# A first set of eight plain products, and the last tokens' turn moved at the border of two mixture layers

## The chip, the cores and the metric

The kernel runs on one core of a Trainium2 chip. The metric is device time in microseconds (us), the median of three runs; the kernel before takes 621.7 us.

The engines are named as in the profile: PE is TensorE (PEld its weight loads), DVE is VectorE, ACT is ScalarE, POOL is GpSimd, SP issues nearly all DMAs. Each engine works through its own queue in the order in which the program emits; semaphores hold an instruction until its operands are there and its output is free.

## The reference, cut to what matters

```python
# 1: retention with decay, batch 2, 8 heads, 576 tokens, head size 64
scores = (q @ k.T) / sqrt(64)
x1 = (scores * Dmat) @ v              # Dmat: gamma_h ** (i - j) for i >= j, else 0
x = x1 to (1152, 512)                 # tokens x model
# 2: four experts of 1024 hidden, weighted by normalized domain_probs
out = sum(p[:, e] * (relu(x @ w1[e]) @ w2[e]) for e in range(4))
# 3: one layer of 2048 hidden, weights in 64-bit floats
h = out @ w_in
y = (h * tanh(softplus(h))) @ w_out   # Mish
```

All is computed in 32-bit precision on TensorE's rounded 32-bit type: each operand is split into a high part (rounded by a copy on ScalarE) and a low part (the rest, by a subtraction), and a product is three matmuls: high x high, low x high, high x low.

## The kernel before

**Retention** (`retention`, L418 to L509). Eight units of one batch and one pair of heads, u = 0 to 7; unit u holds batch u % 2 of pair u // 2. In turn u TensorE computes scores(u), then the values of unit u - 1, the state of unit u, the last scores, and the cross step of unit u - 1. ScalarE scales the keys of unit u + 1 (`prep_k`, L301), copies the state (L363, the first step of `chain`), and places the finished unit in `acc` with its high parts (`place_x`, L403, L411). VectorE does the decay (L332), the rest of the chain (L365) and the low parts (`rest_x`, L416). GpSimd scales the queries of unit u + 1 (`prep_q`, L310, L315). After the loop come the values and the cross step of unit 7. `load_unit` (L273) queues a unit's keys, queries, values and constants (`cst_sb`) on SP.

**Weights.** A chunk (O: first layer, W: second layer) is loaded by `load_w` (L111) into one of three raw buffers and turned into high and low parts by `split_w` (L147): a copy on ScalarE (L153), then four quarter-size subtractions on GpSimd or one on VectorE (L157). A G chunk is made from the raw O chunk by `weight_sums` (L124): four operations on GpSimd (L129 to L132), in place, so its split reads what they leave. `tasks` (L166) is the list of such steps, and `weight_task` (L171) takes the next when it is called and the buffers allow it. In retention it is called once in turns 2, 3 and 6 and twice in turn 5; there it gives O00 split, G00 sums, G00 split, O01 split, G01 sums.

**The two layers** (`feed_forward`, L802). Twelve units of 512 hidden (u = 0 to 7 experts, 8 to 11 the Mish layer), in the order that `steps` (L52) writes out. The first 1024 tokens and the 512 model rows form a 2 x 2 grid of blocks B11, B12, B21, B22; a set S(u, c) (`first_pair`, L609) computes half a unit's hidden layer by seven products on sums of blocks (T1 to T4 of x, G of the weights) in place of eight, and combines them on VectorE and GpSimd. `hidden` (L597) applies ReLU or Mish and splits. The 128 last tokens take a path of their own: L(u, c) (`first_last`, L674), 12 products whose result VectorE transposes in blocks and SP turns by way of DRAM (`turn_rest`, L666, five DMAs). Y(u, c, tb) is a turn of the second layer (`m2`, L754), T(u) the last tokens' (`m2_t`, L779). The second layer's results leave from two PSUM buffers (`ps_tile`, L211) through VectorE (L764, L765).

**The first set** (S(0, 0)) starts inside retention: product 1 runs ahead of the cross step of unit 7 (L488), T sums and splits are spread over turns 3 to 6 and the end (`t_sum`, `t_high`, `t_rest`, L258 to L268).

**The border** lies between u = 7 and u = 8: x of the Mish layer is what the experts leave in `acc`, so its blocks are split (`x_split`, `hi`, `lo`) and its last tokens turned once more, while TensorE goes on to S(8, 0).

The order on each engine is the order of emission (`manual_schedule`, L200).

Of the kernel before, what the change touches and what calls it, by code (L numbers as in the profile page):

```python
# [13 lines left out]
ALU = mybir.AluOpType  # L14
# [5 lines left out]
P = 128  # L20
# [14 lines left out]
CG = 2 * P + D  # L35
KVW = 4 * W4 // P * D + D
CSTW = CG + P + 3
# [11 lines left out]
}  # L49

# [23 lines left out]
def retention_moe_mish(ctx: ExitStack, tc: tile.TileContext, kq_in, kv_in, probs, w1, w2, w64, cdec, out):  # L74
# [10 lines left out]
    order = [(m, 0, c) for m in "OG" for c in range(2)]  # L85
# [61 lines left out]
    def split_w(key, lo_engine, defer=False):  # L147
# [14 lines left out]
        if m != "O":  # L162
            n_raw_max[0] += 1
# [3 lines left out]
    o0, o1, g0, g1 = order[:4]  # L167
    tasks[:6] = [(False, o0), (True, g0), (False, g0), (False, o1), (True, g1), (False, g1)]
# [45 lines left out]
    def product(u, c, n, o):  # L214

        m, kh, fb, r, t, j, opens = PRODUCTS[n]
# [19 lines left out]
    ahead_of = {}  # L236
    early, later = [], []
# [5 lines left out]
    with ExitStack() as actx:  # L243
# [6 lines left out]

        dec_sb = cst_sb[:, :, CSTW - 3:]


        def t_parts(n, kk):
            b11, b12, b21, b22 = (acc[:, i + kk, j * TB:(j + 1) * TB] for i in (0, 2) for j in range(2))
            return {T1: (b11, b12, b11), T3: (b12, b22, b12), T2: (b22, b22, b11), T4: (b21, b21, b22)}[n]

        def t_sum(n, kk):  # L258
            out, a, b = t_parts(n, kk)
            dve.tensor_tensor(out=out, in0=a, in1=b, op=ALU.subtract)  # L260

        def t_high(n, kk):
            act.activation(out=xop[:, 0, n, kk], in_=t_parts(n, kk)[0], func=AF.Copy)

        def t_rest(n, kk):
            dve.tensor_tensor(
                out=xop[:, 1, n, kk], in0=t_parts(n, kk)[0], in1=f32(xop[:, 0, n, kk]), op=ALU.subtract
            )  # L268
# [4 lines left out]
        def load_unit(u):  # L273
# [14 lines left out]
            if b == 0 and u != 4:  # L288
                sp.dma_start(out=cst_sb[:, pr], in_=cdec[pr])
# [50 lines left out]
        def scores_last(u):  # L340
# [5 lines left out]
            for o in own:  # L346
# [3 lines left out]
                in1=cst_sb[:, units[u][1], 2 * P:CG], op=ALU.mult,  # L350
# [47 lines left out]
        def place_x(u, o):  # L398
# [520 lines left out]
```

## Time and profile before

| what | us |
|---|---|
| median of three runs (621.2 to 621.73) | 621.7 |
| the profiled execution | 621.62 |
| its span in the trace | 619.7 |
| TensorE busy in the span | 603.8 |
| VectorE busy | 442.6 |
| GpSimd busy | 377.0 |
| ScalarE busy | 312.9 |

The rows below are lines of one profiled execution. A timeline line gives the start and the length in us, the engine, the line of the kernel, the operation, output and input with shapes, and a count; in brackets stands how long the engine had been idle and what released it. Times count from the start of the span. In lines of the chain a piece is the time that this work held the end of the kernel.

### The profile page before, as it was taken

The page shows a single profiled execution, that of the slowest core. Times are in us where ns is not written, and L with a number is a line of the kernel's source. Part 1 is how long each engine was busy: PE and PEld are TensorE (multiplying, and loading weights), DVE is VectorE, ACT ScalarE, POOL GpSimd, SP SyncE. Part 2 cuts the span into 40 slices and gives each one's busy share as a digit, 9 for nine tenths or more (in the row PEclk, how much of TensorE's full clock was granted, in tenths as well). Part 3 has the DMA queues.
Part 4 walks back from the last instruction along what each step waited for, and adds up shares of the span by engine and source line. Part 5 has one row for each costly group of instructions (what it writes and reads, how often), then busy time and mean ns, then how long its engine had stood idle before and what let it go on. Part 6 is the DMA issues. An engine that isn't in the chain of part 4 may idle for free.

```text
span 619.7 us, 8570 instructions
## 1 busy us (share of the span) xinstructions
PE 603.8 (97%) x3183; PEld 498.5 (80%) x3183; DVE 442.6 (71%) x579; ACT 312.9 (50%) x478; POOL 377.0 (61%) x422
## 2 busy tenths in 40 slices
PE   8999999999999999999999999997899999999997
PEld 7976888888888888888888888875788788888885
DVE  3997768789779779689779779586676867344233
ACT  3676357446446446446446446315656665344120
POOL 2796748758748748758748748663361775854300
PEclk8999999999999999999999999998999999999999
DMA  8933306434523524523524623620220541220023
GB/s 334 400 114 100 120 0 203 121 105 141 162 98 126 152 88 145 175 85 129 160 86 130 195 86 111 178 51 17 48 91 15 172 136 52 85 69 1 0 68 120
DMA packets 56658, 72.30 MB, mean 117 GB/s; under 512 B 31144, under 2 KB 38312, under 8 KB 56616
## 3 DMA queue, kind: packets, MB, share of 16 engines
q1 hardware_dynamic: 56472, 71.46, 36.2%
q8 instruction: 25, 0.41, 0.3%
q10 hardware_dynamic: 144, 0.29, 0.1%
q14 instruction: 17, 0.14, 0.1%
HBM read 57.57 MB, written 14.17 MB: 116 GB/s over the span
## 4 chain that ended last, share of the span: by engine, by line
PE 76%; DVE 10%; DMA 6%; ACT 5%; issue 2%; SPq 1%; POOL 1%; DVEq 0%; ACTq 0%; POOLq 0%
PE b L220 31%; PE ps L695 26%; PE ps L711 14%; PE ps L679 4%; DMA kv<-kv_in 3%; DMA hs<-turned 1%; DMA turned<-hs 1%; DVE x L737 1%; ACT h L601 1%; DVE acc L260 1%; ACT b L600 1%; DVE b L617 1%; SPq L671 1%; DVE h L605 1%; DVE x L416 1%
## 5 line engine op out<-in xcount | busy, mean ns | idle before, releaser
L157 POOL TENSOR_TENSOR w<-wr,w 128x256 fp32r<-128x256 f32 x256 | 216.6, 877 | 119.3 <-ACT w L153 119.3
L220 PE MATMUL b<-x,w 128*128 128x512 f32 x1008 | 243.0, 398 | 7.2 <-DVE x L737 4.7
L220 PEld LDWEIGHTS b<-x,w 128*128 128x128 f32 x1008 | 189.0, 189 | 55.8 <-DVE x L737 6.2
L695 PE MATMUL ps<-h,w 128*128 128x512 f32 x768 | 176.9, 389 | 0.0
L695 PEld LDWEIGHTS ps<-h,w 128*128 128x128 f32 x768 | 143.0, 188 | 29.3 <-issue 0.3
L153 ACT ACTIVATE w<-wr 128x1024 fp32r<-128x1024 f32 x72 | 75.0, 1053 | 29.5 <-POOL wr L132 28.7
L711 PE MATMUL ps<-w,h 128*128 128x512 f32 x384 | 89.1, 390 | 0.3 <-DVE acc L798 0.2
L711 PEld LDWEIGHTS ps<-w,h 128*128 128x128 f32 x384 | 71.4, 188 | 16.0 <-POOL w L157 0.8
L232 ACT ACTIVATE p<-b 128x512 f32<-128x512 f32 x72 | 42.0, 596 | 55.1 <-PE b L220 55.0
L604 ACT ACTIVATE h<-b 128x512 fp32r<-128x512 f32 x64 | 38.2, 597 | 54.4 <-DVE b L617 45.3
L605 DVE SCALAR_TENSOR_TENSOR h<-b,h 128x512 fp32r<-128x512 f32 x64 | 42.7, 689 | 26.2 <-ACT h L604 25.1
L636 POOL TENSOR_TENSOR p<-p,p 128x512 f32<-128x512 f32 x24 | 35.1, 1461 | 36.2 <-ACT p L232 36.2
L764 DVE TENSOR_TENSOR ps<-ps,pb 128x1024 f32<-128x1024 f32 x28 | 34.4, 1229 | 19.3 <-PE ps L695 19.3
L617 DVE TENSOR_TENSOR b<-b,p 128x512 f32<-128x512 f32 x72 | 47.5, 690 | 0.5 <-PE b L220 0.2
L602 DVE TENSOR_TENSOR h<-b,h 128x512 fp32r<-128x512 f32 x32 | 22.1, 690 | 29.3 <-ACT h L601 29.3
L553 ACT ACTIVATE e<-e,cbias 128x512 uint32<-128x512 uint32 x32 | 22.9, 717 | 34.1 <-DVE e L541 34.1
L679 PEld LDWEIGHTS ps<-w,xc 128*128 128x128 f32 x288 | 37.2, 188 | 2.1
L679 PE MATMUL ps<-w,xc 128*128 128x256 f32 x288 | 37.6, 279 | 0.0
L567 DVE TENSOR_TENSOR g<-g,e 128x512 f32<-128x512 f32 x32 | 35.4, 1107 | 1.1
L564 DVE SCALAR_TENSOR_TENSOR g<-w,g 128x512 f32<-128x512 uint32 x32 | 36.0, 1125 | 0.0
L617 DVE TENSOR_TENSOR p<-b,p 128x512 f32<-128x512 f32 x24 | 16.5, 686 | 26.9 <-PE b L220 18.4
L711 PE MATMUL ps<-w,hl 128*128 128x512 f32 x144 | 35.0, 391 | 0.6 <-DVE hl L605 0.6
(81 smaller groups left out, 609.6 us busy)
## 6 DMA issues: line engine op xcount, KB each, us to landing
wr<-w SPq DMA_DIRECT2D x32, 512.0 KB, 5.1
w<-w SPq DMA_DIRECT2D x32, 512.0 KB, 4.5
O<-g SPq DMA_DIRECT2D x16, 256.0 KB, 5.3
W<-g SPq DMA_DIRECT2D x16, 256.0 KB, 4.1
wr<-O SPq DMA_DIRECT2D x8, 512.0 KB, 3.7
wr<-W SPq DMA_DIRECT2D x8, 512.0 KB, 3.3
kq<-kq_in SPq DMA_DIRECT2D x7, 576.0 KB, 9.8
kv<-kv_in SPq DMA_DIRECT2D x7, 544.0 KB, 9.4
```

What stands on the lines that cost most here:

```text
L153: act.activation(out=w[:, 0], in_=t, func=AF.Copy)
L157: lo_engine.tensor_tensor(out=w[:, 1, k], in0=t[:, k], in1=f32(w[:, 0, k]), op=ALU.subtract)
L220: pe.matmul(o[t][j], w[:, a, 2 * kh + kk, fb * P:(fb + 1) * P], xop[:, b, r, kk], start=opens and kk == 0 and i == 0, stop=kk == 1 and i == 2,
L232: act.activation(out=t, in_=src, func=AF.Copy)
L564: dve.scalar_tensor_tensor(out=g, in0=lo_w, scalar=2.0 ** -52, in1=g, op0=ALU.mult, op1=ALU.add)
L567: dve.tensor_tensor(out=g, in0=g, in1=e.bitcast(F32), op=ALU.mult)
L604: act.activation(out=out[:, 0], in_=src, func=AF.Relu)
L605: dve.scalar_tensor_tensor(out=out[:, 1], in0=src, scalar=0.0, in1=f32(out[:, 0]), op0=ALU.max, op1=ALU.subtract)
L617: dve.tensor_tensor(out=out, in0=a, in1=b, op=ALU.add)
L679: pe.matmul(o, xc[:, b, k], w[:, a, k], start=k == 0 and n == 0, stop=k == 3 and n == 2)
L695: pe.matmul(o[:, j], w[:, a, d:d + P], h[:, b, f], start=i == f == n == 0, stop=i == f == 1 and n == 2,)
L711: pe.matmul(o[:, n], h, w[:, b, f * DM:(f + 1) * DM], start=k == f == i == 0, stop=k == f == 1 and i == 2,)
```

## The change

The first set S(0, 0) is computed as eight plain products (list `PLAIN`, `first_plain`) and not as seven on sums. The G weights of this half, the T sums inside retention and the product ahead of the last cross step go; `place_x` also makes the parts of B12, in T4's place. T1, T3, T2, T4 are made from `t_first` around the set. The calls of `weight_task` in turn 3 go, and the list begins O00, O01, G01 sums, G01 split. The first unit's constants are loaded in two pieces, the second behind the keys and queries of unit 1. In every product the two matmuls with the low part of x come last. At the border, L(7, 1) moves into S(7, 1) behind product 6, the last tokens' hidden step ahead of Y(7, 0, 0), no weight is loaded in the steps of Y(7, 0, 0) and Y(7, 0, 1), the split of the turned last tokens goes from Y(7, 1, 1) into S(8, 0) behind product 1, the low part of B21 goes to GpSimd, and S(8, 0) finishes product 3's sums with product 2's.

```diff
+PLAIN = [
+    ("O", 0, 1, B11, 0, 1, True), ("O", 0, 1, T4, 1, 1, True),
+    ("O", 0, 0, B11, 0, 0, True), ("O", 0, 0, T4, 1, 0, True),
+    ("O", 1, 0, B21, 0, 0, False), ("O", 1, 1, B21, 0, 1, False),
+    ("O", 1, 0, B22, 1, 0, False), ("O", 1, 1, B22, 1, 1, False),
+]
...
-    order = [(m, 0, c) for m in "OG" for c in range(2)]
+    order = [("O", 0, 0), ("O", 0, 1), ("G", 0, 1)]
...
-        if m != "O":
+        if m != "O" or key[1:] == (0, 0):
...
-    o0, o1, g0, g1 = order[:4]
-    tasks[:6] = [(False, o0), (True, g0), (False, g0), (False, o1), (True, g1), (False, g1)]
...
-        for kk in range(2):
-            for i, (a, b) in enumerate(((0, 1), (0, 0), (1, 0))):
-                pe.matmul(
-                    o[t][j], w[:, a, 2 * kh + kk, fb * P:(fb + 1) * P], xop[:, b, r, kk],
-                    start=opens and kk == 0 and i == 0, stop=kk == 1 and i == 2,
-                    skip_group_check=not opens,
-                )
+        terms = [(kk, a, 0) for kk in range(2) for a in range(2)] + [(kk, 0, 1) for kk in range(2)]
+        for i, (kk, a, b) in enumerate(terms):
+            pe.matmul(
+                o[t][j], w[:, a, 2 * kh + kk, fb * P:(fb + 1) * P], xop[:, b, r, kk],
+                start=opens and i == 0, stop=i == 5, skip_group_check=not opens,
+            )
...
-                sp.dma_start(out=cst_sb[:, pr], in_=cdec[pr])
+                cs = slice(0, CL) if u == 0 else slice(0, CSTW)
+                sp.dma_start(out=cst_sb[:, pr, cs], in_=cdec[pr, :, cs])
+            if u == 1:
+                sp.dma_start(out=cst_sb[:, pr, CL:], in_=cdec[pr, :, CL:])
             for part in (slice(0, w), slice(w, KVW)) if u == 0 else (slice(0, KVW),):
...
-                if pr >= 2:
-                    parts.append((xop[:, :, B22, kk], x[:, TB:2 * TB]))
+                parts.append((xop[:, :, T4 if pr < 2 else B22, kk], x[:, TB:2 * TB]))
...
             prep_k(0)
+            load_unit(1)
             prep_q(0)
-            load_unit(1)
...
-                for _ in range({2: 1, 3: 1, 5: 1, 6: 1}.get(u, 0)):
+                for _ in range({2: 1, 5: 1, 6: 1}.get(u, 0)):
...
             values(NUN - 1, o)
-            ps = [[None] * 2 for _ in range(2)]
-            ps[0][0] = bank(0, 0)[:, :TB]
-            p = product(0, 0, 1, ps)
-            ahead_of[0, 0] = ps[0][0], p, copy_sum("p1", sums, p)
             rest_x(NUN - 2)
-            for n in (T3, T2, T4):
-                t_sum(n, 0)
             cross(NUN - 1, o)
             place_x(NUN - 1, o)
-            for n in (T3, T2, T4):
-                t_high(n, 0)
             rest_x(NUN - 1)
-            t_sum(T3, 1)
-            t_rest(T3, 0)
...
+    def first_plain(u, c, behind):
+
+        o = [[bank(t, j) for j in range(2)] for t in range(2)]
+        h = [h_tile(u, c, i) for i in range(2)]
+        for i, n in enumerate(PLAIN):
+            t, j, opens = n[-3:]
+            product(u, c, n, o)
+            for f in behind.get(i, ()):
+                f()
+            if not opens:
+                hidden(u, h[t][:, :, j], o[t][j])
...
             elif n == 2 and 7 in done:
+                if 3 in done:
+                    add(done[3], done[3], p16)
                 hidden(u, h[0][:, :, 0], done[2])
+                if 3 in done:
+                    hidden(u, h[1][:, :, 0], done[3])
...
+    def t_first(n):
+        out, x, y = {T1: (b11, b12, b11), T3: (b12, b22, b12), T2: (b11, b22, b11), T4: (b21, b21, b11)}[n]
+        x_minus(out, x, y)
+        hi(n, out)
+        return lambda: lo(n, out)
...
         x_minus(b12, b21, b11)
+        pool.tensor_tensor(out=xop[:, 1, B21], in0=b21, in1=f32(xop[:, 0, B21]), op=ALU.subtract)
 
     def last_t():
         hi(T4, b12)
-        lo(B21, b21)
         lo(T4, b12)
...
-            if (u, c, tb) == (NE - 1, 1, 1):
-                split_x(xc, acc_last, pool)
...
+        rests = [t_first(T1), t_first(T3)]
+        rests.pop(0)()
+
+        def first_t():
+            rests.append(t_first(T2))
+            rests.pop(0)()
+
+        def last_t4():
+            rests.append(t_first(T4))
+            rests.pop(0)()
...
-                    behind = {5: early, 2: [lambda: first_last(u, 0)]}
-                    order = 1, 5, 2, 3, 7, 6, 4
+                    behind = {3: [first_t], 5: [lambda: first_last(u, 0), last_t4]}
+                elif (u, c) == (0, 1):
+                    behind = {1: rests}
+                if (u, c) == (NE - 1, 1):
+                    behind = {6: [lambda: first_last(u, 1)]}
                 if (u, c) == (NE, 0):
-                    behind = {5: [last_x], 7: [last_t], 6: [lambda: first_last(u, 0)]}
+                    behind = {1: [lambda: split_x(xc, acc_last, pool)], 5: [last_x], 7: [last_t]}
+                    behind[6] = [lambda: first_last(u, 0)]
                     order, sum_at = (1, 5, 7, 3, 6, 2, 4), 2
-                elif u == 0:
+                elif (u, c) == (0, 1):
                     later.append(lambda: task(2))
                 elif u == NE:
                     later.append(lambda: task(1))
                     later.append(lambda: task(2, dve))
                 elif c == 1:
                     later.append(task)
-                first_pair(u, c, behind, later, order, sum_at)
+                if (u, c) == (0, 0):
+                    first_plain(u, c, behind)
+                    task(2)
+                else:
+                    first_pair(u, c, behind, later, order, sum_at)
             elif m == "L":
-                first_last(u, *at)
+                if (u, *at) != (NE - 1, 1):
+                    first_last(u, *at)
             elif m == "T":
...
-                if seq[i - 1] == ("Y", u, 0, 0):
+                if seq[i if u == NE - 1 else i - 1] == ("Y", u, 0, 0):
                     hidden(u, hl, hs)
+                if i == i_x:
+                    task()
...
-            if m != "S" and not i_x + 2 <= i <= i_x + 4:
+            if m != "S" and i != i_x and not i_x + 2 <= i <= i_x + 4:
...
-            load_w()
+            if not i_x <= i <= i_x + 1:
+                load_w()
```

## Rows read from the trace of the kernel before

**Rows 1.** The page, part 1: busy us (share of the span) xinstructions

```profile
PE 603.8 (97%) x3183; PEld 498.5 (80%) x3183; DVE 442.6 (71%) x579; ACT 312.9 (50%) x478; POOL 377.0 (61%) x422
```

**Rows 2.** The chain that ended last, in order of time: start us, length us, what

```profile
64.48 10.89 PE ps L695 x48
...
75.38 9.76 PE b L220 x42
...
85.14 1.41 PE ps L679 x12
...
399.61 2.84 DMA hs<-turned
...
449.02 11.14 PE ps L711 x48
```

**Rows 3.** Timeline of ScalarE, 30 to 37: start us, us, instruction

```profile
30.08 1.04 ACT L153 ACTIVATE w<-wr 128x1024 fp32r<-128x1024 f32 x1
...
36.08 0.22 ACT L363 ACTIVATE sbd<-b 128x64 f32<-128x64 f32 x1
```

**Rows 4.** SP queue at 19.67, and the DMA issued there (KB, us to landing)

```profile
19.67 0.33 SPq L121 DMA_DIRECT2D wr<-w  x1
...
wr<-w SPq DMA_DIRECT2D x1, 512.0 KB, 10.8
```

**Rows 5.** Timeline of GpSimd, 31 to 46: start us, us, instruction [idle before <-releaser]

```profile
31.20 3.69 POOL L157 TENSOR_TENSOR w<-wr,w 128x256 fp32r<-128x256 f32 x4 [1.74 <-ACT w L153]
...
34.84 0.86 POOL L310 TENSOR_TENSOR qg<-kq,cst_sb 128x384 f32<-128x384 f32 x1
...
36.99 3.75 POOL L157 TENSOR_TENSOR w<-wr,w 128x256 fp32r<-128x256 f32 x4
...
40.82 1.06 POOL L129 TENSOR_TENSOR wr<-wr 128x256 f32<-128x256 f32 x1
...
44.27 1.27 POOL L132 TENSOR_TENSOR wr<-wr 128x256 f32<-128x256 f32 x1
```

**Rows 6.** Timeline of GpSimd in a steady unit, 351 to 355

```profile
351.30 0.74 POOL L129 TENSOR_TENSOR wr<-wr 128x256 f32<-128x256 f32 x1
...
353.76 0.80 POOL L132 TENSOR_TENSOR wr<-wr 128x256 f32<-128x256 f32 x1
```

**Rows 7.** Timeline of VectorE and TensorE at the last retention unit

```profile
36.50 0.91 DVE L365 SCALAR_TENSOR_TENSOR sbd<-sbd,cst_sb,b 128x64 f32<-128x64 f32 x3
...
39.73 0.99 PE L378 MATMUL ps<-qg,sbd 64*64 64x128 f32 x16
```

**Rows 8.** A window: length, busy us of PE, PEld, DVE, ACT, POOL, PEclk, DMA, GB/s

```profile
424.50:427.70 3.20, 3.11 (x7) 2.48 (x8) 3.17 (x4) 1.42 (x3) 0.00 (x0) 0.50 0.00 0
```

**Rows 9.** The page, part 5: a line's busy us, mean ns, idle before <-releaser

```profile
L153 ACT ACTIVATE w<-wr 128x1024 fp32r<-128x1024 f32 x72 | 75.0, 1053 | 29.5 <-POOL wr L132 28.7
```

**Rows 10.** Timelines at the border of the two stages, 394 to 453

```profile
394.91 2.90 SPq L671 DMA_DIRECT2D turned<-hs  x4
...
403.16 0.73 PE L711 MATMUL ps<-w,hl 128*128 128x512 f32 x2
...
407.00 11.16 PE L695 MATMUL ps<-h,w 128*128 128x512 f32 x48
...
414.01 2.31 SPq L671 DMA_DIRECT2D turned<-hs  x4
...
415.28 2.36 DVE L731 TENSOR_TENSOR acc<-acc 128x1024 f32<-128x1024 f32 x2
...
421.49 0.63 ACT L197 ACTIVATE xc<-acc 128x512 fp32r<-128x512 f32 x1 [10.51 <-DMA acc<-turned]
...
424.59 4.46 PE L220 MATMUL b<-x,w 128*128 128x512 f32 x12 [3.63 <-DVE x L737]
...
442.08 1.05 ACT L153 ACTIVATE w<-wr 128x1024 fp32r<-128x1024 f32 x1
...
449.48 2.83 POOL L157 TENSOR_TENSOR w<-wr,w 128x256 fp32r<-128x256 f32 x4
```

More of the change, by code (lines that the diff above doesn't have):

```diff
@@ L34 @@
 W4 = NCH * P
-CG = 2 * P + D
+CL = 2 * P + 3
+CG = CL + D
 KVW = 4 * W4 // P * D + D
-CSTW = CG + P + 3
+CSTW = CG + P
 B11, B21, B22, T1, T2, T3, T4 = range(7)
@@ L233, in copy_sum @@
         return t
-    ahead_of = {}
-    early, later = [], []
+    later = []
     with ExitStack() as actx:
@@ L249, in retention_moe_mish @@
         sbd_t = [cst.tile([P, NCH, D], F32, name=f"sbd{i}") for i in range(2)]
[L251 to L268, printed above, removed]
+        dec_sb = cst_sb[:, :, 2 * P:CL]
         own = [slice(0, D), slice(D, P)]
@@ L349, in scores_last @@
                 out=ret_t[u][:, 2 * W4:], in0=st[:, w:w + LAST],
-                in1=cst_sb[:, units[u][1], 2 * P:CG], op=ALU.mult,
+                in1=cst_sb[:, units[u][1], CL:CG], op=ALU.mult,
             )
@@ L485, in retention @@
             values(NUN - 1, o)
-            ps = [[None] * 2 for _ in range(2)]
-            ps[0][0] = bank(0, 0)[:, :TB]
-            p = product(0, 0, 1, ps)
-            ahead_of[0, 0] = ps[0][0], p, copy_sum("p1", sums, p)
             rest_x(NUN - 2)
-            for n in (T3, T2, T4):
-                t_sum(n, 0)
             cross(NUN - 1, o)
             place_x(NUN - 1, o)
-            for n in (T3, T2, T4):
-                t_high(n, 0)
             rest_x(NUN - 1)
-            t_sum(T3, 1)
-            t_rest(T3, 0)
-            def rest():
-                for n in (T3, T2, T4):
-                    if n != T3:
-                        t_sum(n, 1)
-                        t_rest(n, 0)
-                    t_high(n, 1)
-                    t_rest(n, 1)
-            early.append(rest)
         retention()
@@ L607, in hidden @@
         )
+    def first_plain(u, c, behind):
[8 more added lines that the diff above has]
+                hidden(u, h[t][:, :, j], o[t][j])
     def first_pair(u, c, behind, later, order, sum_at=7):
-        pre = ahead_of.pop((u, c), None)
-        o = [[pre[0] if pre and t == j == 0 else bank(t, j)[:, :TB] for j in range(2)] for t in range(2)]
+        o = [[bank(t, j) for j in range(2)] for t in range(2)]
         h = [h_tile(u, c, i) for i in range(2)]
@@ L620, in first_pair @@
         for n in order:
-            done[n] = pre[1] if pre and n == 1 else product(u, c, n, o)
+            done[n] = product(u, c, n, o)
             if n == 1:
-                p1 = pre[2] if pre else copy_sum("p1", sums, done[n])
+                p1 = copy_sum("p1", sums, done[n])
             elif n == 5:
@@ L644, in first_pair @@
                 add(done[4], done[4], p16)
-                if 3 in done:
-                    add(done[3], done[3], p16)
                 hidden(u, h[0][:, :, 1], done[4])
@@ L650, in first_pair @@
                     add(done[3], done[3], p16)
-                else:
-                    hidden(u, h[1][:, :, 0], done[3])
                 add(done[6], done[6], p5)
@@ L892 @@
     cdec = np.concatenate([
-        decay[:, 0], decay[:, 1], decay[:, :, :LAST, :LAST].reshape(NPAIR, P, LAST),
+        decay[:, 0], decay[:, 1], np.repeat(gamma ** P, D, axis=1),
+        (gamma ** (P - np.arange(P)) / np.sqrt(D)).swapaxes(1, 2),
+        decay[:, :, :LAST, :LAST].reshape(NPAIR, P, LAST),
         np.repeat(gamma ** np.arange(P), D, axis=1),
-        np.repeat(gamma ** P, D, axis=1),
-        (gamma ** (P - np.arange(P)) / np.sqrt(D)).swapaxes(1, 2),
     ], axis=-1)
```

8 lines of the change are left out of this document (1 added, 7 removed).

## The prediction

> **What bounds the kernel now.** I read the page first: TensorE is busy 97% of the span [rows 1], so time can only come from stretches in which it waits or runs slowly. Second, the chain of work that ended last. In a steady unit it is TensorE alone: a set of 42 products takes 9.76 us (0.232 us each), 12 products of the last tokens 1.41, 48 of the second layer 10.89 [rows 2]. Nothing outside TensorE is on that path, so an edit inside a steady set is worth what it changes in the number of products. Third, the two places where the chain leaves TensorE: the start (up to the first second-layer product at 64.48) and the border between the two stages (up to 449.02) [rows 2]. There I went through each engine's timeline in its queue order, since an engine's next step cannot pass one that waits.
>
> [...] ScalarE stood 10.51 us at the split of the last tokens, whose transposed copy had left the SP queue only at 414.01, behind a weight load; the splits for the first set stood behind it, and TensorE waited 3.63 us [rows 10]. [...]
>
> **The change, part by part.**
>
> *Product order, low part of x last.* The same six matmuls per product, the same weight loads. In a steady set nothing waits on the low part: 0. Where a low part comes late it gives four matmuls (0.93 us) of grace.
>
> *First constants load cut, the rest behind the second unit's keys.* Some 0.2 us earlier for the first state, which is lost again: the end of retention hangs on GpSimd, below. 0.
>
> *First set plain.* It adds one product of six: 48 x 0.232 = 11.15 us against 9.76, so +1.4. It removes the T sums and their splits from the retention loop, the sums and split of one weight chunk (G of the first half), the first product ahead of the last cross step, and all the combining adds. Its first four products (5.6 us) read only pieces that units 0 to 3 left, so the last unit's copies and splits hide behind them; T1, T3, T2, T4 are now made during the set and are needed only by the second one. If nothing else moved, the last cross step would start at 38.2, right behind the values of unit 7, and 1.0 for it, 11.15, twice 1.41 and 9.76 put the second layer at 62.9 instead of 64.48: -1.5.
>
> But a weight task moves. The task list now reads O00, O01, G01 sums, G01 split. Unit 2 takes the first, unit 5 the second and third, unit 6 the fourth. Before, unit 6 held the sums of G01, on GpSimd alone; now it holds the split, whose first step is a ScalarE copy that reads what GpSimd's sums leave. That copy stands in ScalarE's queue ahead of the last unit's state copy (L363), and so of the chain that feeds the last cross step. When GpSimd is done:
> - O01 is issued at 19.67 and lands 10.8 later, at 30.47 [rows 4]. Its ScalarE copy can start at 30.5; GpSimd follows a copy's start by 1.12 (30.08 to 31.20) [rows 3, 5]: 31.6.
> - Four low parts, 3.69 to 3.75 there [rows 5], 3.3 at the spacing of GpSimd operations in a steady unit (0.82, 351.30 to 353.76 over three) [rows 6]. I take 3.3: 34.9.
> - The query scalings of units 6 and 7, 34.84 to 36.99 before [rows 5]: 2.15, so 37.1. The cross step of unit 6 waits for the first of them; so TensorE is at the end of retention no earlier than now, and the values of unit 7 end near 38.2, as now (39.73 less the product ahead of it).
> - Four sums: 40.82 to 45.54 before, 4.7 [rows 5]; 3.3 in a steady unit [rows 6]. VectorE, blocked behind the state copy, has nothing to do then, so I take 3.3: 40.4.
> - ScalarE's copy takes 1.05 [rows 9], so the state copy starts at about 41.4; from its start to the end of the decay chain it was 36.08 to 37.41, 1.3 [rows 3, 7]: 42.7. The cross step starts there and not at 39.73 [rows 7].
>
> TensorE is thus idle from 38.2 to 42.7. After the 3.63 us wait at the border the clock was down for 3.2 us [rows 8, 10]; so I count 1.6 here. Then 42.7 + 1.0 (cross) + 1.6 + 11.15 + 2 x 1.41 + 9.76 = 69.1, against 64.48: **+4.6**. Low end: low parts and sums at the steady price, copy and chain as above and no fall of the clock: +3.0. High end: low parts 3.75, sums 4.7: +1.9 more, +6.5.
>
> [...] GpSimd's four sums went at 0.82 spacing in one place and 1.18 in the other [rows 5, 6]. [...]
>
> *The border.* (a) The last tokens' products of unit 7 move into the set, behind product 6. TensorE reaches the T step at 403.1 now [rows 10]; two turns before it (10.9) and the three products left (4.2) put the end of the last tokens' products at 388.0. I allow 2 for what VectorE has queued, so their transposed copy leaves SP near 390 and not at 394.91; it came back at 402.45 (399.61 + 2.84) [rows 2, 10], 7.5 later, so now at 397.5 to 398.5, behind the load that shares the queue. Their hidden step now stands ahead of the first second-layer turn's evictions on ScalarE and VectorE; at most 2.4 for it (one copy and one subtraction, half the size of L731, 2.36 for two) and two evictions at L731's 1.2 each [rows 10] free the buffer for the T step by 402.3 to 403.3; TensorE gets there at 403.1. The T step then runs 403.1 to 405.8 (12 products at 0.227), and the next turn starts there, not at 407.00 [rows 10]: -1.2.
> (b) Without the weight load ahead of it the second transposed copy goes out near 407.6, as soon as VectorE has written it, and is back 7.5 later, at 415. The set of unit 8 starts at 416.8, and ScalarE's split of the last tokens stands behind the splits for it. Each large VectorE step is 1.2: from the end of the turn before the last at 411.3 the low part of T3 is ready at 417.4 (used at 419.5), B22 at 418.7, T2 at 422.4 (used at 422.3, its low part 0.93 later), T4 at 425.9 (used at 426.5). The low part of B21 goes to GpSimd behind its high part (422.3), at most the 3.3 of four quarters [rows 6]: 425.6, wanted at 426.0. So the 3.63, the slow clock (1.6) and the small waits between go; TensorE runs from 416.8 to product 1 of the next set at 429.3 unbroken.
> (c) What is late next: banks. The second set's products 7 and 6 wait for the Mish chains of the first, about 0.2 and 1.2 (before, product 5 waited 1.09 [rows 10]): it ends at 440.4.
> (d) Then weights: the second half's low part came 10.2 us after ScalarE's copy of the first half (442.08 to 449.48 + 2.83 = 452.31) [rows 10]; that copy now starts near 434.2, so 444.4, and TensorE wants it at 443.1: 1.3.
> Second layer done: 440.4 + 10.9 + 1.3 = 452.6, against 449.02 + 11.14 = 460.16 [rows 2]: **-7.5**. Check from the other side: 416.8 to 440.4 is 23.6 for 84 + 24 products, 22.3 without a wait. Bounds: -8.5 if neither bank nor weight waits as long, -6 if the transposed copy is 1.5 late.
> The skipped weight load follows one step later and is used some 25 us on: 0. After the border both kernels run the same tasks in the same steps.
>
> **Sum.** The profiled execution took 621.62 (span 619.7), 0.08 under the median of 621.7. +4.6 - 7.5 = -2.9; from the median, 618.8.
>
> **Rivals.**
> 1. *ScalarE is not held* (the sums are done when the split's turn comes, or the state copy can go ahead): start -1.5, border -7.5, 612.7. For it: the chunk's GpSimd work is four operations shorter. Against: the two scalings and four low parts stand ahead in GpSimd's queue, and ScalarE does stand for this pair now, 28.7 us in all [rows 9]. [...] Chance 0.10.
> 2. *Slower:* the last tokens' hidden step, now ahead of the evictions of the first second-layer turn. If their copy comes back later than about 398.7, VectorE frees the T step's buffer too late, and TensorE waits one for one. Back at 402.45 as now, it ends its low part at 404.4, both evictions at 406.9: 3.8 of waiting and 1.6 of slow clock, so the border gives 2.1, and the time is 621.7 + 4.6 - 2.1 = 624.2. Against it: the copy leaves 5 us earlier. Chance 0.10.
> 3. *The border's gain turns into a weight wait:* if step (d) slips by 2.5 (ScalarE's copies wait for the bank chains, GpSimd for adds before the weights), -5 and 621.3. For it: the low part came just in time before. Chance 0.12.
>
> **How the numbers follow.** Forecast 0.68, its own range 616.3 to 621.0; the rivals 0.10, 0.10, 0.12. About 0.2%, 1.25 us, is what a measurement of this kernel tells from no change: under 620.45 is faster, over 622.95 slower. Faster: most of the forecast (0.60), rival 1, a little of rival 3: 0.73. Same: the rest of the forecast and of rival 3: 0.17. Slower: 0.10. The range 615.0 to 622.4 leaves out rival 1 and the slower rival.
>
> **What would show it.** Right: TensorE idle from about 38 to 43, the cross step there released by VectorE's decay chain, ScalarE standing some 4 us at the weight copy for GpSimd's sums, a clock of 0.50 behind it, the second layer first at 69; at the border no wait of ScalarE for the transposed copy, none of TensorE over 1.5 us, PEclk 1.00 throughout, the second layer of unit 8 done within 13 us of its set's end. Wrong: a cross step before 41 (rival 1), a T step that starts after 404 (rival 2), a wait over 2.5 in the second layer of unit 8 (rival 3).

## The result, and the profile after

The changed kernel takes 615.53 us (median of four runs, 615.09 to 616.25), the kernel before beside it 621.45 (620.44 to 621.73): a ratio of 0.9911, with a 95% interval of 0.9899 to 0.9923. The medians lie 5.9 us apart; the interval, taken of 621.45, is 4.8 to 6.3 us. The forecast was 618.8. The direction and the two places were right; the gain is twice what was foretold (5.9 for 2.9).

The profiled execution took 615.17 us with a span of 613.3. Its first page, and TensorE's waits (line waited for: us in total, times, longest):

```profile
PE 601.5 (98%) x3189; PEld 500.7 (82%) x3189; DVE 430.6 (70%) x568; ACT 310.6 (51%) x472; POOL 368.7 (60%) x413
...
PE ps L370 <- ACT sbd L355: 3.7, 1, 3.7
PE b L227 <- DVE h L568: 1.6, 2, 0.9
```

TensorE's busy time fell from 603.8 [rows 1] to 601.5, and the longest wait that is left is the 3.7 us of the last cross step, at the start. The span falls into five stretches, read from TensorE's timeline: to the first turn of the second layer, to Y(7,0,0), to the second layer of unit 8, to the end of the last matmul, to the end of the span (a timeline starts that first turn 0.16 us ahead of the chain of [rows 2]).

| stretch, us | before | after | difference |
|---|---|---|---|
| start, to Y(0,0,0) | 64.32 | 66.92 | +2.60 |
| experts, to Y(7,0,0) | 327.88 | 327.44 | -0.44 |
| border, to the second layer of unit 8 | 56.66 | 49.15 | -7.51 |
| Mish layer, to the last matmul's end | 166.80 | 166.20 | -0.60 |
| end of the span | 4.04 | 3.59 | -0.45 |
| span | 619.70 | 613.30 | -6.40 |

**The start.** The timelines of ScalarE, GpSimd, VectorE and TensorE (start us, us, engine, line, instruction, [idle before <-releaser]); L162 is the weight copy (L153 before), L138 to L141 the four sums, L355 the state copy, L357 VectorE's part of the decay chain, L370 the cross step:

```profile
29.32 1.06 ACT L162 ACTIVATE w<-wr 128x1024 fp32r<-128x1024 f32 x1 [0.33 <-DMA wr<-w]
...
39.31 1.06 ACT L162 ACTIVATE w<-wr 128x1024 fp32r<-128x1024 f32 x1 [4.47 <-POOL wr L141]
40.27 0.21 ACT L355 ACTIVATE sbd<-b 128x64 f32<-128x64 f32 x1
```

```profile
30.45 3.25 POOL L166 TENSOR_TENSOR w<-wr,w 128x256 fp32r<-128x256 f32 x4 [4.70 <-ACT w L162]
33.67 1.00 POOL L302 TENSOR_TENSOR qg<-kq,cst_sb 128x384 f32<-128x384 f32 x1
...
36.15 0.72 POOL L138 TENSOR_TENSOR wr<-wr 128x256 f32<-128x256 f32 x1
...
38.55 0.72 POOL L141 TENSOR_TENSOR wr<-wr 128x256 f32<-128x256 f32 x1
```

```profile
40.51 0.91 DVE L357 SCALAR_TENSOR_TENSOR sbd<-sbd,cst_sb,b 128x64 f32<-128x64 f32 x3 [5.21 <-ACT sbd L355]
```

```profile
35.85 1.09 PE L385 MATMUL ps<-ret,kv 128*64 128x128 f32 x16
40.62 1.76 PE L370 MATMUL ps<-qg,sbd 64*64 64x128 f32 x16 [3.68 <-ACT sbd L355]
...
66.92 11.09 PE L671 MATMUL ps<-h,w 128*128 128x512 f32 x48
```

The reader sees the forecast's chain: the copy of G01 stands 4.47 us for GpSimd's sums, the state copy stands behind it, and TensorE waits for that. The granted clock of the window behind it (length, busy us of PE, PEld, DVE, ACT, POOL, PEclk, DMA, GB/s) is lower:

```profile
40.00:42.00 2.00, 1.38 (x14) 1.41 (x16) 1.42 (x5) 1.65 (x4) 1.56 (x3) 0.62 0.01 4
42.00:45.00 3.00, 3.00 (x18) 2.44 (x15) 3.00 (x5) 1.48 (x3) 1.74 (x2) 0.69 0.32 96
```

**The border.** TensorE (L687 the last tokens' turn, L671 a turn of the second layer, L227 the set), then SP, ScalarE's split of the last tokens, and the clock over the whole of it. These lines answer to [rows 10] and [rows 8]:

```profile
405.29 2.88 PE L687 MATMUL ps<-w,hl 128*128 128x512 f32 x12
408.12 11.16 PE L671 MATMUL ps<-h,w 128*128 128x512 f32 x48
419.12 7.11 PE L227 MATMUL b<-x,w 128*128 128x512 f32 x30
...
435.28 1.66 PE L227 MATMUL b<-x,w 128*128 128x512 f32 x6 [0.67 <-DVE h L568]
437.86 5.82 PE L227 MATMUL b<-x,w 128*128 128x512 f32 x24 [0.92 <-DVE h L568]
443.51 3.61 PE L687 MATMUL ps<-w,h 128*128 128x512 f32 x15
447.28 7.78 PE L687 MATMUL ps<-w,h 128*128 128x512 f32 x33 [0.15 <-POOL w L166]
```

```profile
409.92 1.95 SPq L647 DMA_DIRECT2D turned<-hs  x4
```

```profile
421.27 0.62 ACT L204 ACTIVATE xc<-acc 128x512 fp32r<-128x512 f32 x1
```

```profile
412.00:442.00 30.00, 28.41 (x135) 23.10 (x134) 21.61 (x23) 18.62 (x27) 12.10 (x9) 1.00 0.16 39
```

The wait of 3.63 and the 10.51 of ScalarE [rows 10] are gone, the clock is 1.00 in every window from 388 to 450, and the stretch is 7.51 us shorter.

### The profile page after: what moved, and what is told of

It reads as the page before. It is cut to its first block, busy times and chain, and to the rows that moved or that the text cites. A ratio compares the mean times of both kernels' runs of the same rounds, so it can differ in the third digit from the quotient of the medians.

```text
span 613.3 us, 8553 instructions
## 1 busy us (share of the span) xinstructions
PE 601.5 (98%) x3189; PEld 500.7 (82%) x3189; DVE 430.6 (70%) x568; ACT 310.6 (51%) x472; POOL 368.7 (60%) x413
## 4 chain that ended last, share of the span: by engine, by line
PE 83%; DMA 5%; POOL 4%; DVE 3%; issue 2%; ACT 2%; SPq 0%; POOLq 0%; DVEq 0%
PE b L227 33%; PE ps L671 28%; PE ps L687 17%; PE ps L655 5%; DMA kq<-kq_in 2%; DMA wr<-w 2%; POOL w L166 1%; DMA cst_sb<-cdec 1%; DMA w<-w 1%; POOL p L616 1%; POOL x L728 1%; POOL qg L302 0%; DVE acc L745 0%; ACT h L567 0%; DVE ps L744 0%
## 5 line engine op out<-in xcount | busy, mean ns | idle before, releaser
L166 POOL TENSOR_TENSOR w<-wr,w 128x256 fp32r<-128x256 f32 x252 | 214.0, 882 | 135.1 <-ACT w L162 135.1
L227 PE MATMUL b<-x,w 128*128 128x512 f32 x1014 | 240.8, 395 | 2.0 <-DVE h L568 1.6
L227 PEld LDWEIGHTS b<-x,w 128*128 128x128 f32 x1014 | 190.3, 188 | 47.2 <-DVE h L568 2.5
L671 PE MATMUL ps<-h,w 128*128 128x512 f32 x768 | 177.0, 389 | 0.0
L671 PEld LDWEIGHTS ps<-h,w 128*128 128x128 f32 x768 | 143.2, 188 | 29.4 <-issue 0.3
L687 PE MATMUL ps<-w,h 128*128 128x512 f32 x384 | 88.6, 390 | 0.2 <-POOL w L166 0.2
L162 ACT ACTIVATE w<-wr 128x1024 fp32r<-128x1024 f32 x71 | 73.8, 1053 | 27.3 <-POOL wr L141 27.0
L687 PEld LDWEIGHTS ps<-w,h 128*128 128x128 f32 x384 | 71.6, 188 | 15.2 <-POOL w L166 0.6
L238 ACT ACTIVATE p<-b 128x512 f32<-128x512 f32 x69 | 40.6, 598 | 52.9 <-PE b L227 52.7
L593 DVE TENSOR_TENSOR b<-b,p 128x512 f32<-128x512 f32 x69 | 45.7, 691 | 2.5 <-POOL p L617 2.0
L744 DVE TENSOR_TENSOR ps<-ps,pb 128x1024 f32<-128x1024 f32 x28 | 34.4, 1229 | 16.5 <-PE ps L671 16.4
L745 DVE TENSOR_TENSOR acc<-acc,ps 128x1024 f32<-128x1024 f32 x28 | 34.2, 1221 | 1.0
L687 PE MATMUL ps<-w,hl 128*128 128x512 f32 x144 | 34.6, 389 | 0.0
```

Source lines behind the costliest of these rows:

```text
L162: act.activation(out=w[:, 0], in_=t, func=AF.Copy)
L166: lo_engine.tensor_tensor(out=w[:, 1, k], in0=t[:, k], in1=f32(w[:, 0, k]), op=ALU.subtract)
L227: pe.matmul(o[t][j], w[:, a, 2 * kh + kk, fb * P:(fb + 1) * P], xop[:, b, r, kk], start=opens and i == 0, stop=i == 5, skip_group_check=no ...
L238: act.activation(out=t, in_=src, func=AF.Copy)
L593: dve.tensor_tensor(out=out, in0=a, in1=b, op=ALU.add)
L671: pe.matmul(o[:, j], w[:, a, d:d + P], h[:, b, f], start=i == f == n == 0, stop=i == f == 1 and n == 2,)
```

## The experiments

Each was timed beside the kernel before. The stretches in this table are those of the table above, in us, each from one profiled execution. The start scatters between executions of the same start (66.92 to 68.57) and the times with it, while the border's stretch came within 0.03 in the four executions that share the changed border (49.15 to 49.18). So the border is compared by its stretch.

| kernel | time / before | interval | start | experts | border | Mish layer |
|---|---|---|---|---|---|---|
| product order alone | 1.0000 | 0.9991 to 1.0009 | 63.98 | 327.46 | 56.30 | 166.28 |
| border alone | 0.9874 | 0.9861 to 0.9887 | 64.68 | 327.88 | 49.59 | 166.45 |
| start and order | 1.0038 | 1.0024 to 1.0051 | 68.46 | 327.45 | 56.50 | 166.07 |
| changed, G01 split behind | 0.9847 | 0.9832 to 0.9862 | 63.41 | 327.44 | 49.15 | 166.31 |
| changed, again | 0.9921 | 0.9902 to 0.9940 | 68.18 | 327.44 | 49.18 | 166.08 |
| changed, constants whole | 0.9929 | 0.9913 to 0.9944 | 67.10 | 327.44 | 49.15 | 166.19 |
| changed, last turn a step of its own | 0.9937 | 0.9924 to 0.9950 | 67.87 | 327.45 | 50.22 | 166.11 |
| changed, loads back | 0.9919 | 0.9902 to 0.9935 | 68.57 | 327.44 | 49.15 | 166.10 |
| changed, split back | 0.9934 | 0.9921 to 0.9947 | 68.15 | 327.44 | 50.12 | 166.18 |
| changed, loads and split back | 0.9944 | 0.9925 to 0.9963 | 67.88 | 327.44 | 50.77 | 166.05 |
| changed, weight step back | 0.9957 | 0.9941 to 0.9973 | 68.12 | 327.44 | 51.26 | 166.30 |
| changed, loads, split and weight step back | 1.0058 | 1.0040 to 1.0075 | 67.92 | 327.44 | 56.69 | 166.13 |

### The change in three parts

The kernel before with the new order of the matmuls in `product` alone:

```diff
-        for kk in range(2):
-            for i, (a, b) in enumerate(((0, 1), (0, 0), (1, 0))):
...
+        terms = [(kk, a, 0) for kk in range(2) for a in range(2)] + [(kk, 0, 1) for kk in range(2)]
```

> The kernel before with the new order of the six matmuls in a product, nothing else. As forecast, the order is worth nothing in a steady set: 621.4, within 0.1%. The rival, from the two traces (a set of 42 products 9.73 us in the kernel after against 9.76 before): 23 sets of 0.03 to 0.045, so 0.7 to 1.0 us faster, 620.5, and the sets in this run take 9.73.

Measured: 621.06 beside 620.85, no difference. Its trace shows that the order does something all the same: the experts' stretch is 0.42 shorter, as in every kernel with this order (327.44 to 327.46, against 327.88 in both without it). A set of 42 takes 9.73 us and not the 9.76 of [rows 2]; 14 sets make 0.42. It is less than a timing of this kernel resolves, so the order is not shown to give time by itself.

The kernel before with the border's edits alone (the moved L(7,1), hidden step, weight step and split, the skipped loads, B21's low part on GpSimd, product 3's sums):

> The kernel before with the border's edits alone, old product order and old start. Forecast for the border: 7.5 us faster, 613.9, and the second layer of unit 8 ends at 452.6. If the border's gain rests on the new product order (low parts of x used last), TensorE waits up to 0.9 us each for the low parts of T2 and T4, and it is 5.5 to 6.5.

Measured: 612.96 beside 620.85, -7.8 (-7.0 to -8.6); the border's stretch is 49.59 against 56.66. The gain does not rest on the product order.

The changed kernel with the border undone, that is start and order alone:

> The kernel after with the border undone: the plain first set, the changed start and the product order. By the trace of the kernel after the second layer begins 2.6 us later than before (67.1 against 64.5), and the order gives 0.7 to 1.0 back: 1.6 to 1.9 us slower than the kernel before, 623.2. By the forecast's own term for the start (+4.6, order nothing): 626.0.

Measured: 623.25, +2.4 (+1.5 to +3.2). So the start costs time, as the forecast had it, and the border gives all of the gain: 0.9874 x 1.0038 = 0.9911, the whole. The profiled execution of this kernel has a later start than that of the changed kernel, with the same instructions and the same queues in front of it:

```profile
30.80 1.06 ACT L162 ACTIVATE w<-wr 128x1024 fp32r<-128x1024 f32 x1 [0.29 <-DMA wr<-w]
...
40.76 1.06 ACT L162 ACTIVATE w<-wr 128x1024 fp32r<-128x1024 f32 x1 [4.89 <-POOL wr L141]
```

```profile
42.08 1.45 PE L370 MATMUL ps<-qg,sbd 64*64 64x128 f32 x16 [3.76 <-ACT sbd L355]
```

The load of the second O chunk came 1.5 us later, and the cross step behind it moved with it. This execution, 624.54, is one of the slower of the six of this kernel (621.97 to 624.57).

### Does the copy of G01 hold the start?

The changed kernel with the task of turn 6 issued behind the last unit's copies:

```diff
-                for _ in range({2: 1, 5: 1, 6: 1}.get(u, 0)):
+                for _ in range({2: 1, 5: 1}.get(u, 0)):
...
             place_x(NUN - 1, o)
+            weight_task(-1, pool)
             rest_x(NUN - 1)
```

> The kernel after with one weight task moved: G01's split no longer in turn 6 of retention but behind the copies of the last unit. If ScalarE's stand for GpSimd's sums is what holds the last cross step (3.68 us, then a slow clock to 44), the cross step follows the values of unit 7 at about 36.9, the clock stays at 1.00, and the second layer begins at 36.9 + 1.0 + 11.1 + 2.8 + 9.7 = 61.5 to 62.6 instead of 67.1: 4.5 to 5.5 us faster than the kernel after, 610 to 611. The rival, that another wait lies right behind it (the chain through VectorE, the scaled queries of unit 7, or the T sums that now fall earlier): under 2 us, 613.5 or more, with a wait of TensorE in the first set.

Measured: 611.28 beside 620.85, the fastest of all, just above the 610 to 611 of the expectation and well under the rival's 613.5. The load came late here too (the expectation had counted on an early one, with the cross step at 36.9), and the cross step was not held for it:

```profile
30.65 1.06 ACT L162 ACTIVATE w<-wr 128x1024 fp32r<-128x1024 f32 x1 [1.29 <-DMA wr<-w]
...
35.77 0.20 ACT L355 ACTIVATE sbd<-b 128x64 f32<-128x64 f32 x1
...
41.50 1.06 ACT L162 ACTIVATE w<-wr 128x1024 fp32r<-128x1024 f32 x1 [0.74 <-POOL wr L141]
```

```profile
38.09 0.99 PE L370 MATMUL ps<-qg,sbd 64*64 64x128 f32 x16
```

```profile
40.00:42.00 2.00, 2.00 (x10) 1.62 (x9) 1.73 (x3) 1.26 (x3) 1.39 (x2) 1.00 0.49 176
```

The state copy comes at 35.77 and not at 40.27, the cross step starts right behind the values, at 38.09 (the forecast's "if nothing else moved" was 38.2), and the clock stays at 1.00 in every window from 36 to 48. So the wait and the slow clock are the work of one weight task's place, by the rows above of its ScalarE copy. Against the border alone this kernel is 612.96 - 611.28 = 1.7 us faster, with ranges that overlap (610.33 to 613.22 and 612.70 to 614.14). That is the plain first set once it is not held and the product order together. In the trace the start alone is 63.41, against 63.98 to 64.68 with the old start: 0.6 to 1.3 less, where the prediction had 1.5 for the plain set.

### How fixed is the start?

The changed kernel once more:

> The changed kernel once more, beside the run above, for a second view of its start. Theory: the last cross step starts 11.3 us after ScalarE's copy of the second O chunk starts, as in six executions so far (11.28 to 11.30), and that start hangs on the landing of the chunk's load, which has come at 29.3 to 30.8; so the cross step lies between 40.6 and 42.1 and the time between 615 and 617. Rival: the landing is fixed by the queue order, 29.3 in this kernel; cross step at 40.6, time 615.5 within 0.4.

Measured: 616.09 beside 621.05. The copy of the chunk started at 29.58 and the cross step at 40.87. By itself this is close to both expectations; the ten executions that have this start settle it (in one of them the constants are loaded whole). The copy started between 29.32 and 30.80, each time released by the landing of the load, and the cross step 11.27 to 11.30 behind it, between 40.62 and 42.08. The first turn of the second layer came at 66.92 to 68.57, 68.0 in the middle: +3.7 against the 64.3 of the three executions with the old start. The +2.60 of the table is the earliest of the ten.

And the constants in one piece:

```diff
-                cs = slice(0, CL) if u == 0 else slice(0, CSTW)
+                cs = slice(0, CSTW)
...
-            if u == 1:
-                sp.dma_start(out=cst_sb[:, pr, CL:], in_=cdec[pr, :, CL:])
```

> The changed kernel with the first unit's constants loaded in one piece ahead of the first values, as in the kernel before. Theory of the forecast: the first state starts some 0.2 us later, but TensorE waits at the end of retention for GpSimd and ScalarE, whose times hang on the load of the second O chunk; no difference, 615.5 within 0.5. Rival: the values of unit 0 land later, and the queue behind them with them, so that the second O chunk lands later too and the last cross step with it: 616.2 to 617.5.

Measured: 616.75 beside 620.57; the interval overlaps that of the changed kernel. Copy at 29.43, cross step at 40.72: within what repeats give. The profiled execution was the fastest of the six (615.36 to 617.48), and the slower ones have no trace. No difference is shown, and the rival's later landing is not excluded for them.

### What carries the border?

L(7,1) as a step of its own again, and the hidden step behind Y(7,0,0):

```diff
-                if (u, c) == (NE - 1, 1):
-                    behind = {6: [lambda: first_last(u, 1)]}
...
-                if seq[i if u == NE - 1 else i - 1] == ("Y", u, 0, 0):
+                if seq[i - 1] == ("Y", u, 0, 0):
```

> The changed kernel with the last tokens' products L(7,1) back as a step of their own behind the set, and their hidden step back behind Y(7,0,0). Theory of the forecast, part (a): their transposed copy comes some 4 us later, the T step of unit 7 waits, and its stretch from the T step's start to the next turn is 1.2 us longer than the 2.8 of the changed kernel: 616.7, from 616.3 to 617.3. Rival 1, the move is hidden anyway: 615.5 within 0.4. Rival 2, the wait is followed by a stretch at the lower clock: over 618.

Measured: 617.08, as part (a) had it; the stretch is 1.07 longer. The T step waits inside itself, as it did before [rows 10], and the next turn starts 3.81 behind its start and not 2.83:

```profile
406.31 0.73 PE L687 MATMUL ps<-w,hl 128*128 128x512 f32 x2
407.64 2.56 PE L687 MATMUL ps<-w,hl 128*128 128x512 f32 x10 [0.60 <-DVE hl L571]
410.12 11.16 PE L671 MATMUL ps<-h,w 128*128 128x512 f32 x48
```

The weight loads back in the steps of Y(7,0,0) and Y(7,0,1):

```diff
-            if not i_x <= i <= i_x + 1:
-                load_w()
+            load_w()
```

> The changed kernel with the weight loads put back into the steps of Y(7,0,0) and Y(7,0,1). Theory, each of two edits enough by itself: with the load ahead, SP stands until GpSimd is done with the raw buffer (410.3 in the changed kernel, where the copies are ready at 409.9), so the last tokens' second copy leaves 0.4 us late and shares the queue with 512 KB; it is back near 418, and ScalarE's split of it, now behind product 1 of S(8,0) at 421.3, still waits for nothing. Time as the changed kernel's 615.5, within 0.6. Rival, the skipped load carries the gain: SP stands until about 414 as in the kernel before, the copy is back after 421.5, ScalarE and the high part of B21 behind it are late, TensorE waits over 1 us in S(8,0) and the time is 617 to 619.

Measured: 616.46, above the expectation (the profiled start is late, 68.57), and the stretch is 49.15, to the hundredth that of the changed kernel. The copy left SP 18.1 us behind the start of Y(7,0,0) and not 15.6, and its split, behind product 1 of S(8,0), still waited for nothing. The skipped loads are worth nothing by themselves.

The split of the turned last tokens back in Y(7,1,1):

```diff
+            if (u, c, tb) == (NE - 1, 1, 1):
+                split_x(xc, acc_last, pool)
...
-                    behind = {1: [lambda: split_x(xc, acc_last, pool)], 5: [last_x], 7: [last_t]}
+                    behind = {5: [last_x], 7: [last_t]}
```

> The changed kernel with ScalarE's split of the turned last tokens put back ahead of the high parts of T3, B22 and T2 (in Y(7,1,1)), weight loads still out of the way. Theory, each of two edits enough by itself: the copy leaves at 409.9 and is back at 416.2, ScalarE splits it at 416.3 to 416.9, and the high part of T3 waits for VectorE's sum until 417.6 anyway. No wait of TensorE over 1 us in S(8,0), time 615.5 within 0.6. Rival, the place of the split carries the gain: ScalarE comes late to T3, TensorE stands at product 3 or 4 of S(8,0) and runs at the lower clock behind it, 617 to 620.

Measured: 616.89, stretch 50.12: +0.97, between the two expectations. ScalarE stood 3.74 us for the copy; TensorE lost time in pieces of 0.2 to 0.3, with the clock at 1.00 throughout.

Both together:

> The changed kernel with both edits of the last two border runs together: the weight loads back in the steps of Y(7,0,0) and Y(7,0,1), and the split of the turned last tokens back ahead of the high parts of T3, B22 and T2. The load alone left the stretch from Y(7,0,0) to the second layer of unit 8 as it is (49.15 us), the split alone made it 1.0 longer. Theory, each edit was enough against the same wait: with the load ahead the copy is back some 3.8 us later than without (as that run shows), ScalarE stands for it, T3's high part comes about 3 us late, TensorE waits 2 to 3.6 us in S(8,0) and runs at the lower clock behind it, as in the kernel before: the stretch is 53 to 55, and the time 619.0 to 621.0. Rival, the two prices only add: 50.2 and 616.5.

Measured: 617.51, stretch 50.77: +1.62. My theory fell, and the rival (the two prices add) was nearer. The copy left SP at 411.65, 16.3 us behind the start of Y(7,0,0), where the kernel before needed 21.8 (414.01 [rows 10] less 392.20). SP stands for a raw buffer, and something else had freed it 5.5 us earlier. The timeline of GpSimd names it: the four sums (L138 the first) stood ahead of the low part of B11 (L205) and no longer behind it.

```profile
401.95 1.07 POOL L138 TENSOR_TENSOR wr<-wr 128x256 f32<-128x256 f32 x1
...
405.99 2.41 POOL L205 TENSOR_TENSOR x<-acc,x 128x1024 fp32r<-128x1024 f32 x1 [0.52 <-ACT x L204]
```

That is the weight step of Y(7,0,0), which the change issues ahead of the turn's own work:

```diff
-                if i == i_x:
-                    task()
...
-            if m != "S" and i != i_x and not i_x + 2 <= i <= i_x + 4:
+            if m != "S" and not i_x + 2 <= i <= i_x + 4:
```

With this undone as well (the moved L(7,1), the low part of B21 on GpSimd and product 3's sums stay as in the change):

> As the run with both edits undone (weight loads back, split of the last tokens back), and with the weight step of Y(7,0,0) back behind that turn's own work too, so that GpSimd's four sums stand behind its low part of B11 again. Theory, three edits against one wait: the sums start some 11.7 us behind the start of Y(7,0,0) and not 6.6, ScalarE's weight copy follows them at 15.3 and not 10.5, GpSimd frees the raw buffer near 21, and SP, standing behind the load for that buffer, sends the last tokens' second copy at 21.5 to 22 and not 16.3; ScalarE stands for it and TensorE waits 2 us or more in S(8,0) with the lower clock behind: the stretch from Y(7,0,0) to the second layer of unit 8 is 54 to 56, the time 619.5 to 621.5. Rival, the place of the weight step matters nothing: 50.8 as with two undone, and the rest of the border's gain lies in the low part of B21 and in the sums of product 3: 617 to 618.

Measured: 624.37, 1.0058 of the kernel before, and the stretch is 56.69, as long as before (56.66). Time and stretch lie above the theory's ranges, and the rival, that the place of the weight step matters nothing, fell. GpSimd, ScalarE, SP and TensorE, and the clock behind:

```profile
406.12 2.39 POOL L205 TENSOR_TENSOR x<-acc,x 128x1024 fp32r<-128x1024 f32 x1 [4.18 <-ACT x L204]
408.47 0.74 POOL L138 TENSOR_TENSOR wr<-wr 128x256 f32<-128x256 f32 x1
```

```profile
412.62 1.06 ACT L162 ACTIVATE w<-wr 128x1024 fp32r<-128x1024 f32 x1 [6.58 <-POOL wr L141]
...
425.45 0.63 ACT L204 ACTIVATE xc<-acc 128x512 fp32r<-128x512 f32 x1 [10.82 <-DMA acc<-turned]
```

```profile
417.61 0.32 SPq L130 DMA_DIRECT2D wr<-O  x1
418.02 2.32 SPq L647 DMA_DIRECT2D turned<-hs  x4
```

```profile
420.12 2.96 PE L227 MATMUL b<-x,w 128*128 128x512 f32 x12
427.08 2.70 PE L227 MATMUL b<-x,w 128*128 128x512 f32 x6 [4.00 <-ACT x L722]
```

```profile
428.00:432.00 4.00, 3.78 (x9) 2.17 (x8) 3.96 (x5) 1.90 (x3) 0.00 (x0) 0.50 0.00 0
432.00:436.00 4.00, 4.00 (x18) 3.31 (x17) 2.87 (x4) 3.18 (x4) 2.79 (x1) 0.66 0.02 4
```

ScalarE's 10.51, TensorE's 3.63 and the clock of 0.50 of the kernel before [rows 8, 10] have come back as 10.82, 4.00 and 0.50. Both kernels wait behind the first 12 matmuls of S(8,0). That the two stretches agree to 0.03 is chance: the T step here does not wait (2.83 to the next turn, 3.84 before), and the clock was low for some 6.8 us (an estimate from 0.50 in 428 to 432 and 0.66 in 432 to 436), where it was low for some 3.4 before (0.50 in 424.5 to 427.7 [rows 8]). What the low clock added to the stretch is open. The old border does not need it to be that long: with the product order alone TensorE waited 2.17 us at the same place and then in smaller pieces, its matmuls behind the wait took 1.19 us for 4 and 2.59 for 10, where 12 took 4.46 in [rows 10], and the stretch was 56.30.

```profile
422.33 1.19 PE L220 MATMUL b<-x,w 128*128 128x512 f32 x4 [2.17 <-ACT x L739]
```

And the weight step alone put back, loads and split as in the change:

> The changed kernel with only the weight step of Y(7,0,0) back behind that turn's own work. Theory, the three edits stand in for each other: no load stands ahead of the last tokens' second copy and their split is late, so the stretch stays at 49.2, up to 49.8 if the weights of unit 8 come later with it; time 615 to 616.5. Rival, the place of the weight step carries the gain by itself: over 52, 618 to 620.

Measured: 618.26, stretch 51.26: +2.11, between theory and rival. The copy of the last tokens goes out in time here (411.12), and yet TensorE loses 2.1 us. By the trace it is the mechanism of the start once more: ScalarE's weight copy stands for the sums, and a split of x, VectorE's low part of it and the evictions stand behind it (timelines of ScalarE and VectorE, L204 and L205 the split, L744 an eviction, at 413.88 in the changed kernel, which is 1.2 us ahead of this one here):

```profile
413.65 1.06 ACT L162 ACTIVATE w<-wr 128x1024 fp32r<-128x1024 f32 x1 [6.58 <-POOL wr L141]
414.61 1.04 ACT L204 ACTIVATE x<-acc 128x1024 fp32r<-128x1024 f32 x1
```

```profile
415.69 1.61 DVE L205 TENSOR_TENSOR x<-acc,x 128x1024 fp32r<-128x1024 f32 x1 [3.49 <-ACT x L204]
417.23 1.22 DVE L744 TENSOR_TENSOR ps<-ps,pb 128x1024 f32<-128x1024 f32 x1
```

The three edits thus overlap in one gain: undone alone they cost 0 (loads), 0.97 (split) and 2.11 (weight step), loads and split 1.62, all three 7.54, more than their sum of 3.08. The other two pairs were not run, and neither were the low part of B21 and product 3's sums by themselves: whether these carry anything is not shown.

## Why the prediction was wrong in size

**The step that failed is the sum's start term, and beside it the terms set to nothing.** Foretold were +4.6 and -7.5, -2.9 in all; the whole is -5.9 (in the repeat -5.0). By the stretches, with the start at the middle of its ten executions: +3.7 - 0.44 - 7.51 - 0.60 - 0.45 = -5.3.

*Start, +4.6 foretold; +3.7 in the middle of ten traces (+2.6 to +4.2), +2.4 as timed with the order (+1.5 to +3.2).* The mechanism is the one foretold, link by link: GpSimd 1.13 behind the copy (1.12 taken), low parts to 33.67, 3.22 (3.3), sums from 36.15 to 39.31, 3.16 (3.3), copy 0.96 (1.05). VectorE ran nothing from 35.31 to 40.51, as foretold; that this gave the sums their short price was the author's estimate and is not shown (last section). Two links were mis-sized. The scalings took 2.48 (2.15). And from the state copy's start to the cross step it was 0.35, where I had put 1.3, the whole of VectorE's decay chain: the chain ran from 40.51 to 41.42 while the cross step's matmuls had started at 40.62, released by ScalarE. From the chunk's copy to the cross step I had 12.2; it is 11.3 every time. Then I took the landing of the load from one execution, 30.47 [rows 4]; it was up to 1.2 earlier in others. The slow clock, 1.6 in the sum, came out at 1.57 here, the longer cross step (1.76 for 0.99) included (26.30 from the cross step to Y(0,0,0) less the 24.73 of the sum); without the wait the same steps took 24.83 (15.11 to the second set with the split behind, and 9.72 for that set here).

*Terms of nothing.* The product order gives 0.03 us per set, -0.44 over the experts. The Mish layer and the end of the span, "the same tasks in the same steps", are 0.60 and 0.45 shorter. Order and border each show some of the first alone (166.28 and 166.45 against 166.80). The end took 3.5 to 3.7 in the changed kernel (twice) and in eight made from it, and 3.8 to 4.9 in the four others. What shortens either was not settled.

*Constants: 0.* Nothing else is shown.

*Border, -7.5 foretold; -7.51 in the trace, -7.8 as timed.* The sum is right, in part by luck, and (a) with it (1.07 for 1.2). In (b) the copy left SP 15.56 behind the start of Y(7,0,0), for the 15.4 taken (407.6 less 392.20). But the reason given, that no weight load stands ahead of it, is not what carries it: with the load in place nothing is lost. The weight step's place, which the prediction did not price, frees the raw buffer early enough for the split where the change has it. Nor is the 1.6 of slow clock at the old border shown to be a cost of its own: with the product order alone no matmuls were slow like that behind its wait (10 in 2.59 us), and the border took 56.30 for 56.66. Parts (c) and (d) erred against each other: the banks cost 1.6 and not 1.4, the weights 0.15 and not 1.3; from the set's start to the second layer of unit 8 it was 24.4 and not 23.6.

*Rivals.* The first (ScalarE not held) was wrong of this kernel and right of its price: the kernel in which it is not held is at 611.28, 9.6 below its before, where the rival had -9.0. The second did not come: the last tokens' copy was back 5.8 us behind the start of Y(7,0,0), and the T step 10.93 behind it, without a wait. The third did not come either, with a weight wait of 0.15. Two of the signs as written came true without their rivals: the cross step came before 41 in four of the ten executions (40.62 to 40.90), by an early load and with ScalarE held all the same, and the T step started at 405.29, after 404, because the start came later. And what released the cross step was ScalarE's state copy, not VectorE's chain.

## What to carry to other kernels

On an engine that works in order, price a moved step by what then stands behind it: here one ScalarE copy that waits for GpSimd's sums cost about 4 us at the start and about 2 at the border, and issuing it later, or the sums earlier, gave them back. Undoing one of several edits against the same wait shows little of what they give together, so undo them in pairs and all together before a gain is put down to one. And a chain that hangs on a load should be sized from more than one execution, with each link's true releaser: here the cross step started 0.80 us ahead of the end of the decay chain, which had been taken for what it waits for.

## What the runs showed of the hardware

One 512 KB load landed at times 1.5 us apart (29.3 to 30.8, by the start of the copy that it released) in ten executions, in nine of them behind the same loads on the same queue. In the changed kernel its issue came at 19.85, and it took 9.4 from there; in the kernel before it took 10.8 [rows 4]. The last cross step followed it each time by 11.27 to 11.30.

The slow clock behind the same wait of 3.7 us is not of one length. In the changed kernel the granted clock of 42 to 45 was 0.69; in its repeat the windows read

```profile
42.00:45.00 3.00, 3.00 (x17) 2.47 (x15) 3.00 (x5) 1.48 (x3) 1.98 (x3) 0.50 0.28 62
45.00:48.00 3.00, 3.00 (x12) 2.32 (x11) 2.96 (x4) 1.30 (x2) 0.00 (x0) 0.78 0.95 187
```

From the cross step to Y(0,0,0) it took 26.3 to 27.3 us over the ten, 1.4 to 2.5 more than the 24.83 without the wait: that is what one such wait cost beyond itself.

GpSimd's operations of one shape did not take one time. Its four sums took 0.72 each in the changed kernel while VectorE ran nothing (L138 to L141 above), 1.06 to 1.27 in [rows 5] with VectorE busy 4.73 of the 4.80 us from 40.8 on, and 0.74 to 0.80 in [rows 6] with VectorE busy 3.27 of the 3.30 us from 351.3 on; with the split behind they took 1.18, 1.07, 0.74 and 0.74. So the short price, which the prediction took for a blocked VectorE, came beside a busy one too. The four low parts of the border's weight took 2.83 in the changed kernel, 3.81 and 3.82 in the two kernels with the weight step behind that turn's own work, 4.88 before. What sets these times was not shown.
